# Small transfers of the normalisation and of the filter taps issued by GpSimd, filter taps written in pieces of 16 partitions, and the order of the work made with other costs

## The chip, the cores and the metric

The kernel runs on one core of a Trainium2 chip, whose cores have five engines with queues of their own: TensorE (PE, with its weight loads shown apart as PEld), VectorE (DVE), ScalarE (ACT), GpSimd (POOL) and SyncE (SP). Each engine executes its instructions strictly in the order in which they were written, and waits at an instruction until the semaphores named there have their values. A DMA is issued by an engine's queue (here SP, ACT or POOL) and carried out by the core's 16 DMA engines. The metric is the device time of one execution in microseconds; lower is better.

## The reference

The input `x` is 2048 positions by 448 channels, bf16. The result mixes an attention branch `a` and a state-space convolution branch `b` with a gate `g` of each position:

```
x = A_x
g = _sigmoid((x * gate_w).sum(-1, keepdims=True))
a = _A_ref(x, A_wq, A_wk, A_wv, A_wo)
b = _B_ref(x, B_A_re, ..., B_log_dt, B_Dskip)
return g * a + (1 - g) * b
```

`_A_ref` is attention with 16 heads of 28 channels that share one set of keys and values: `softmax(q k^T / sqrt(28)) v`, then a product with `wo`. `_B_ref` makes a filter `K` of 2048 taps for each of the 448 channels, from 256 complex states, and convolves each channel of `x` causally with its filter (there by FFT):

```
logdA = dt * A
P = jnp.exp(logdA[:, :, None] * l[None, None, :])
K = jnp.einsum("dn,dnl,dn->dl", Cc, P, dB).real
...
y = (lambda x, *d: x.transpose(*d))(y, 0, 2, 1) + u * Dskip[None, None, :]
```

## The kernel before

**Attention** runs in 16 rounds: round i takes a block of 512 queries (i // 4) and a group of four heads (i % 4). In a round, 64 score tiles of 128 keys by 512 queries are made by TensorE (L1031, into the PSUM tensor `psS`), exponentiated by ScalarE in sets of two or three tiles (L1047, `expT`), and multiplied with the values by TensorE (L1056), which adds up in the one PSUM bank `psB`. The values have a column of ones, so that one row of `psB` per head is the softmax denominator. At a round's end `norm(i)` copies `psB` to `acc` (L947, DVE), which frees `psB` for the next round. Then four DMAs gather the denominators (`denT<-acc`), DVE takes reciprocals (L952), one DMA writes them to a DRAM scratch (`R_scratch<-denT`), four read them back spread over partitions (`rdenB<-R_scratch`), and DVE multiplies (L956, `onT<-acc,rdenB`). `acc` is single, so L956 of a round has to come ahead of L947 of the next. The last round, 15, does this with TensorE instead. After rounds 3, 7, 11 and 15 the output projection with `wo` follows (L930, L997) and is added to the output `O` in SBUF (L939).

**The convolution** goes through 14 blocks c of 32 channels. DVE builds tables of powers for a block (`masters` and `tables`, L736 to L834), TensorE makes the taps from them (`kgen`, L851), DVE copies these to `kstg` (L861, L864), and DMAs write `kstg` to the DRAM scratch `KP_scratch` (slot name `kw`). The taps are read back as Toeplitz tiles: each block has two calls of `conv`, with four tiles each, 112 tile loads in all (`T<-KP_scratch`, 1072 KB each, in `tload`), into four buffers of `T`. TensorE multiplies a tile with `U`, the rearranged input (L893, 32 matmuls for each tile), DVE scales the result of a `conv` (L902, `cst`), TensorE transposes it (L913), and DVE adds it to `O` (L921).

**The order.** The code first lists all operations with their dependences, an estimated duration and a priority. `Prog.schedule` then plays them through with these estimates and so sets one fixed order for each engine; `emit` writes it out with the semaphore waits. A transfer's estimate is its own duration, plus `DMA_NS` (2200 ns), plus `extra`; transfers share one time line `dmafree`, and their issuer is held for 500 ns for each DMA. All DMAs that the prediction speaks of are issued by SP, whose queue is as strict as that of the other engines: a tile load behind an issue that waits is not issued either.

In the profile, every DMA has line 128 (`e.dma_start` in `Prog.dma`), so DMAs are told apart by their tensors. POOL does only early work: constants and the 16 copies that make `U` (L495).

## Time and profile before

| | us |
|---|---|
| median of 3 runs (641.67 to 643.77) | 643.0 |
| the profiled execution itself | 646.27 |
| its span in the profile | 644.5 |
| first exponential of the attention | 30.2 |
| copy of `acc` of the first and of the last round | 65.7 and 597.4 |
| last taps copied to `kstg` | 537.2 |

The profile gives for each engine the time in which it was busy, for each wait the engine and line that ended it, and a row for each instruction or run of like instructions with its start, its duration and the idle time ahead of it in brackets. The mean granted TensorE clock was 0.72 of the full clock. Slices in which the engines are busy do not tell which of them sets the pace, since three of them are busy for three quarters of the span or more; the waits do.

### The profile page before, as it was taken

The numbers are of one execution on the slowest core, as the hardware profiler recorded it, in microseconds if no ns is written. First come the engines' busy times: TensorE is split into PE (matmuls) and PEld (weight loads), VectorE is DVE, ScalarE is ACT, GpSimd is POOL, SyncE is SP. The second block draws the span as 40 slices with busy tenths as digits, with TensorE's granted clock in tenths as the row PEclk, the third lists the DMA queues.
The fourth block names the chain that finished last, engine by engine and source line by source line (L and its number), as shares of the span: only waits on it lengthen the run. The fifth ranks groups of instructions, "written<-read, shape, count | busy, mean of one in ns | idle before, by whom it ended". The sixth has DMA issues, their size and how long they took to land.

```text
span 644.5 us, 18460 instructions
## 1 busy us (share of the span) xinstructions
PE 516.5 (80%) x8219; PEld 224.3 (35%) x8234; DVE 471.0 (73%) x1028; ACT 490.6 (76%) x427; POOL 23.3 (4%) x36
## 2 busy tenths in 40 slices
PE   6598788889689776869689879798997888899642
PEld 5231132434233332424232434243341434343431
DVE  8989998989788896959778988969795961010310
ACT  4689998979779795959678979878796989787000
POOL 2740000000000000000000000000000000000000
PEclk9755585959789795958777976767596879555855
DMA  9510006496657148494672747593948172999695
GB/s 271 136 29 2 17 7 243 132 395 236 229 212 262 38 152 339 103 396 164 254 261 68 289 126 312 179 410 105 386 151 319 45 253 73 404 392 344 270 421 200
DMA packets 48686, 139.03 MB, mean 216 GB/s; under 512 B 25360, under 2 KB 31056, under 8 KB 34272
## 3 DMA queue, kind: packets, MB, share of 16 engines
q1 hardware_dynamic: 47952, 137.30, 58.7%
q8 instruction: 64, 1.05, 0.6%
q10 hardware_dynamic: 656, 0.57, 0.3%
q14 instruction: 14, 0.11, 0.0%
HBM read 133.81 MB, written 3.91 MB: 214 GB/s over the span
## 4 chain that ended last, share of the span: by engine, by line
DMA 32%; DVE 24%; PE 20%; ACT 11%; SPq 9%; issue 2%; ACTq 0%
DMA denT<-acc 14%; ACT expT L1047 11%; SPq L128 9%; DMA T<-KP_scratch 7%; PE psS L1031 7%; DMA R_scratch<-denT 5%; DMA rdenB<-R_scratch 4%; PE psB L1056 4%; DVE tab L812 3%; PE psX L893 2%; PE psS L893 2%; DVE tmp L814 2%; DVE tab L818 2%; DVE tab L816 2%; DVE tab L814 1%
## 5 line engine op out<-in xcount | busy, mean ns | idle before, releaser
L1047 ACT ACTIVATE expT<-psS 128x1536 bf16<-128x1536 f32 (+1 forms) x410 | 475.6, 1269 | 89.9 <-PE psS L1031 88.0
L1031 PE MATMUL psS<-qT,kT 29*128 29x512 bf16 x1024 | 202.9, 493 | 38.6 <-ACT expT L1047 30.5
L1056 PE MATMUL psB<-expT,vaug 128*32 128x512 bf16 x1024 | 129.1, 495 | 1.0 <-DVE acc L947 1.0
L1031 PEld LDWEIGHTS psS<-qT,kT 29*128 29x128 bf16 x1024 | 40.6, 95 | 135.9 <-ACT expT L1047 90.6
L893 PE MATMUL psX<-T,U 128*18 128x128 bf16 (+7 forms) x1792 | 50.2, 262 | 33.0 <-DMA T<-KP_scratch 24.6
L812 DVE TENSOR_TENSOR tab<-tab,mbf 128x256 bf16<-128x256 bf16 (+4 forms) x70 | 68.4, 977 | 0.3
L893 PE MATMUL psS<-T,U 128*18 128x128 bf16 (+7 forms) x1792 | 55.7, 273 | 15.4 <-DMA T<-KP_scratch 15.1
L1056 PEld LDWEIGHTS psB<-expT,vaug 128*32 128x32 bf16 x1024 | 27.3, 97 | 87.5 <-issue 84.2
L893 PEld LDWEIGHTS psX<-T,U 128*18 128x18 bf16 (+7 forms) x1792 | 35.8, 112 | 50.7 <-DMA T<-KP_scratch 29.4
L851 PE MATMUL psX<-tab 128*32 128x64 bf16 x1280 | 50.8, 290 | 2.6 <-DVE tab L834 2.5
L893 PEld LDWEIGHTS psS<-T,U 128*18 128x18 bf16 (+7 forms) x1792 | 38.8, 115 | 36.7 <-issue 15.0
L952 DVE RECIPROCAL denT<-denT 128x16 f32<-128x16 f32 x15 | 3.8, 252 | 58.4 <-DMA denT<-acc 58.4
L851 PEld LDWEIGHTS psX<-tab 128*32 128x32 bf16 x1280 | 36.8, 138 | 19.3 <-issue 13.3
L814 DVE TENSOR_TENSOR tmp<-tab,mbf 128x256 bf16<-128x256 bf16 (+3 forms) x56 | 36.3, 649 | 0.0
L947 DVE COPY acc<-psB 128x512 f32<-128x512 f32 x16 | 11.0, 685 | 31.4 <-PE psB L1056 31.3
L829 DVE TENSOR_TENSOR tab<-tab,tmp 128x4096 bf16<-128x4096 bf16 x14 | 31.9, 2282 | 0.0
L814 DVE TENSOR_TENSOR tab<-tab,mbf 128x4096 bf16<-128x4096 bf16 x14 | 31.9, 2276 | 0.0
L902 DVE TENSOR_TENSOR cst<-psX,omq 128x512 bf16<-128x512 f32 x14 | 9.6, 686 | 26.4 <-PE psX L893 26.3
L736 DVE TENSOR_TENSOR msq<-mst 128x256 f32<-128x256 f32 x63 | 26.2, 415 | 0.0
L825 DVE TENSOR_TENSOR tmp<-tmp,mbf 128x64 bf16<-128x64 bf16 (+4 forms) x70 | 25.0, 357 | 0.4
L816 DVE TENSOR_TENSOR tab<-tab,tmp 128x128 bf16<-128x128 bf16 (+3 forms) x56 | 22.4, 400 | 0.2
L818 DVE TENSOR_TENSOR tab<-tab,tmp 128x128 bf16<-128x128 bf16 (+3 forms) x56 | 22.3, 399 | 0.0
(139 smaller groups left out, 458.9 us busy)
## 6 DMA issues: line engine op xcount, KB each, us to landing
T<-KP_scratch SPq DMA_DIRECT2D x112, 1072.0 KB, 8.7
rdenB<-R_scratch SPq DMA_DIRECT2D x60, 64.0 KB, 2.2
tab<-in_A_x_dram SPq DMA_DIRECT2D x4, 448.0 KB, 6.0
tab<-in_A_x_dram SPq DMA_DIRECT2D x16, 112.0 KB, 2.6
out_dram<-O SPq DMA_DIRECT2D x3, 448.0 KB, 3.8
denT<-acc SPq DMA_DIRECT2D x60, 2.0 KB, 6.7
KP_scratch<-kstg SPq DMA_DIRECT2D x56, 17.0 KB
tab<-in_A_x_dram SPq DMA_DIRECT2D x16, 56.0 KB, 6.3
```

The lines of the kernel that those rows point to most:

```text
L128: return [e.dma_start(o, i, **kw) for o, i in pairs]
L736: pg.op("dve", lambda e, k=k: e.tensor_tensor(msq.v(0, P, 0, [[BW, 2], [1, BW]]), both(k - 1), both(k - 1), ALU.mult), el(2 * BW), rd=keys ...
L812: vo(lambda e, dst=dst, src=src, mr=mr: e.tensor_tensor(dst, src, mr, ALU.mult), 2 * n, done + mk(lv), [kr, ki])
L814: vo(lambda e, src=src, mi=mi, w=w, tb=tb, to=to: e.tensor_tensor(tb.v(0, P, to, [[w * EW, 2], [EW, w], [1, EW]]), src, mi, ALU.mult), 2 * ...
L816: vo(lambda e, do=do, n=n, tb=tb, to=to: e.tensor_tensor(tab.v(0, P, do, [[1, n]]), tab.v(0, P, do, [[1, n]]), tb.v(0, P, to + n, [[1, n]] ...
L818: vo(lambda e, do=do, n=n, tb=tb, to=to: e.tensor_tensor(tab.v(0, P, do + BLK, [[1, n]]), tab.v(0, P, do + BLK, [[1, n]]), tb.v(0, P, to, ...
L829: vo(lambda e: e.tensor_tensor(tab.v(0, P, FM, [[64, 2], [EW, 32], [1, 64]]), tab.v(0, P, lo + 31 * EW, [[BLK, 2], [-EW, 32], [1, 64]]), r ...
L851: r = e.matmul(G.v(32 * g, 32, 64 * jj, [[1, 64]]), tab.v(0, P, lo + comp * BLK + 64 + o, [[EW, 32]]), tab.v(0, P, fo, [[mo - fo, 2], [EW, ...
L893: r = e.matmul(ps.v(32 * j, 32 - 2 * n, 128 * k, [[1, 128]]), self.U.v(0, P, (4 * gi + j) * 32 + 2 * n, [[1, 32 - 2 * n]]), self.T.v(0, P, ...
L1031: r = e.matmul(self.psS.v(0, P, 512 * (bo + k), [[1, 512]]), kT.v(32 * h, DH + 1, 128 * kt, [[1, 128]]), qT.v(32 * h, DH + 1, 512 * (i % 2 ...
L1047: pg.op("act", lambda e: e.activation(expT.v(0, P, 512 * es, [[1, n]]), self.psS.v(0, P, 512 * bo, [[1, n]]), AF.Exp, scale=SQ), 100 + n / ...
L1056: r = e.matmul(self.psB.v(32 * h, 32, 0, [[1, 512]]), vaug.v(0, P, 32 * kt, [[1, 32]]), expT.v(0, P, 512 * (t % RING), [[1, 512]]), start= ...
```

## The change

The change has four parts. The tap writes `KP_scratch<-kstg` and the three transfers of the normalisation are issued by POOL instead of SP. The tap writes are cut otherwise: before, eight pieces, of which four have 17 partitions and four have 16; now eight pieces of 16 partitions, and one that carries row 16 of each of the four groups (32 runs of 64 taps). The scheduler's estimates are others: a POOL issue holds its engine for 1000 ns, a transfer of POOL doesn't wait for the transfers ahead of it, four transfers have 2000 ns more of latency, a tile load 2500 ns in place of 1500, the taps' matmuls 235 ns in place of 285, and four matmuls of the convolution 58 ns in place of 70. So the order of every engine is made anew. What is computed stays the same.

```diff
             if o.slot is not None:
-                free[e] = r + 500.0 * o.ndma
-                s = max(r, dmafree)
-                dmafree = s + o.ns
-                end = dmafree + self.DMA_NS + o.extra
+                free[e] = r + (1000.0 if e == "pool" else 500.0) * o.ndma
+                s = r if e == "pool" else max(r, dmafree)
+                end = s + o.ns + self.DMA_NS + o.extra
+                dmafree = max(dmafree, s) + o.ns
...
-                pg.op("pe", lambda e, mm=mm, comp=comp: mm(e, comp), 285, mode="c", rd=keys,
+                pg.op("pe", lambda e, mm=mm, comp=comp: mm(e, comp), 235, mode="c", rd=keys,
...
-        lst = []
+        ko = self.kstg
+        rs = ko.rs
+        lst = [(dram(self.KP, 32 * c * KW + 1024, [[8 * KW, 4], [KW, 8], [1, 64]]),
+                bass.AP(tensor=ko.h, offset=16 * rs, ap=[[32 * rs, 4], [64, 8], [1, 64]]))]
         for g in range(4):
-            for h, (r0, nr) in enumerate(((0, 17), (16, 16))):
-                lst.append((dram(self.KP, h * KH + (32 * c + 8 * g) * KW, [[64, nr], [KW, 8], [1, 64]]),
-                            self.kstg.v(32 * g + r0, nr, 0, [[64, 8], [1, 64]])))
-        pg.dma(lst, (1056, 128), "kw", rd=["kst", "kst2"], wr=[("KP", c)], pr=0)
+            for h in range(2):
+                lst.append((dram(self.KP, h * KH + (32 * c + 8 * g) * KW, [[64, 16], [KW, 8], [1, 64]]),
+                            ko.v(32 * g + 16 * h, 16, 0, [[64, 8], [1, 64]])))
+        pg.dma(lst, (1056, 128), "kw", rd=["kst", "kst2"], wr=[("KP", c)], pr=0, eng="pool", extra=2000)
...
-               (128, 2 * TW), f"T{s}", rd=[("KP", gi // 8), "pad"] + x, wr=[("T", s)], pr=1, extra=1500)
+               (128, 2 * TW), f"T{s}", rd=[("KP", gi // 8), "pad"] + x, wr=[("T", s)], pr=1, extra=2500)
...
-                pg.op("pe", mm, 70, mode="c", rd=[("T", s)] + [("U", q) for q in range(4)],
+                pg.op("pe", mm, 58, mode="c", rd=[("T", s)] + [("U", q) for q in range(4)],
...
-                   (128, 64), "dn", rd=["acc"], wr=["dn"], pr=0)
+                   (128, 64), "dn", rd=["acc"], wr=["dn"], pr=0, eng="pool", extra=2000)
...
-            pg.dma([(dram(self.R, i * 2048, [[16, P], [1, 16]]), dv)], (128, 64), "rw", rd=["dn"], wr=[("R", i)], pr=0)
+            pg.dma([(dram(self.R, i * 2048, [[16, P], [1, 16]]), dv)], (128, 64), "rw", rd=["dn"], wr=[("R", i)], pr=0, eng="pool", extra=2000)
...
-                   (128, 2048), "rdb", rd=[("R", i)], wr=["rd"], pr=0)
+                   (128, 2048), "rdb", rd=[("R", i)], wr=["rd"], pr=0, eng="pool", extra=2000)
```

The diff moves lines behind L864 down by three: L893 is L896 after the change, L902 is L905, L921 is L924, L947 is L950, L952 is L955, L956 is L959, L1031 is L1034, L1047 is L1050, L1056 is L1059.

**First place: the issuing queues.** SP's queue before, from the reciprocals' write of one round to the taps of the block behind it:

```order
L128 DMA R_scratch<-denT 128x16
L128 DMA rdenB<-R_scratch 32x512 x4
L128 DMA T<-KP_scratch 128x1x4288
L128 DMA KP_scratch<-kstg 17x8x64
L128 DMA KP_scratch<-kstg 16x8x64
```

The last two rows stand four times in turn before the next tile load. POOL's queue now, behind the copies that make `U`, for one round and the start of the next:

```order
L128 DMA denT<-acc 32x1x16 x4
L128 DMA R_scratch<-denT 128x16
L128 DMA rdenB<-R_scratch 32x512 x4
L128 DMA KP_scratch<-kstg 32x1x64
L128 DMA KP_scratch<-kstg 16x8x64 x8
L128 DMA denT<-acc 32x1x16 x4
```

These rows repeat to the end of POOL's queue. SP's queue holds the 112 tile loads one behind the other, from the first to the last, and behind them the output.

**Second place: DVE between the copy of `acc` and the reciprocal of the second round** (i = 1). Before:

```order
L947 COPY acc<-psB 128x512
L713 CAST qT<-psS 128x512
L814 TENSOR_TENSOR tab<-tab,mbf 128x4096
L952 RECIPROCAL denT<-denT 128x16
L816 TENSOR_TENSOR tab<-tab 128x2048
L818 TENSOR_TENSOR tab<-tab 128x2048
```

Now, from the row right behind the copy of `acc` on:

```order
L713 CAST qT<-psS 128x512
L814 TENSOR_TENSOR tab<-tab,mbf 128x4096
L821 COPY tmp<-mbf 128x64
L816 TENSOR_TENSOR tab<-tab 128x2048
L818 TENSOR_TENSOR tab<-tab 128x2048
L825 TENSOR_TENSOR tmp<-tmp,mbf 128x64
L825 TENSOR_TENSOR tmp<-tmp,mbf 128x128
L779 CAST mbf<-seedq 128x2x64
L825 TENSOR_TENSOR tmp<-tmp,mbf 128x256
L779 CAST mbf<-qst 128x2x64
L825 TENSOR_TENSOR tmp<-tmp,mbf 128x512
L955 RECIPROCAL denT<-denT 128x16
```

Nine rows of table work have moved ahead of this round's reciprocal. In other rounds it is fewer rows than before: the order now puts about the same amount of work there in every round.

**Third place: DVE's last instructions**, from the copy of `acc` of the last round on. `cst` is written once for each `conv`. Before:

```order
L947 COPY acc<-psB 128x512
L968 RECIPROCAL denT<-psS 128x16
L970 COPY rdenB<-denT 128x512
L979 TENSOR_TENSOR onT<-acc,psS 128x512
L902 TENSOR_TENSOR cst<-psS,omq 128x512
L939 SCALAR_TENSOR_TENSOR O<-psS,gt,O 128x448 x2
L921 TENSOR_TENSOR O<-O,psS 128x16x16
L939 SCALAR_TENSOR_TENSOR O<-psS,gt,O 128x448
L939 SCALAR_TENSOR_TENSOR O<-psX,gt,O 128x448
L921 TENSOR_TENSOR O<-O,psS 128x16x16
L902 TENSOR_TENSOR cst<-psX,omq 128x512
L921 TENSOR_TENSOR O<-O,psS 128x16x16
```

Two more pairs of L902 and L921 follow. Now the whole rest is:

```order
L950 COPY acc<-psB 128x512
L971 RECIPROCAL denT<-psS 128x16
L973 COPY rdenB<-denT 128x512
L905 TENSOR_TENSOR cst<-psX,omq 128x512
L982 TENSOR_TENSOR onT<-acc,psS 128x512
L942 SCALAR_TENSOR_TENSOR O<-psS,gt,O 128x448 x4
L924 TENSOR_TENSOR O<-O,psS 128x16x16
L905 TENSOR_TENSOR cst<-psX,omq 128x512
L924 TENSOR_TENSOR O<-O,psS 128x16x16
```

Before, the results of four calls of `conv` are taken up behind the last copy of `acc`; now those of two. On PE, 476 of the 3584 matmuls of L893 stood behind the last one of L1056 before, and 192 do now.

## The prediction

> **What bounds the kernel now.** I read the page's first part, then the rounds of attention, then who waits for whom. No engine is full, and three are nearly even:
>
> ```profile
> span 644.5 us, 18460 instructions
> PE 516.5 (80%) x8219; PEld 224.3 (35%) x8234; DVE 471.0 (73%) x1028; ACT 490.6 (76%) x427; POOL 23.3 (4%) x36
> ```
>
> The copies of `acc`, one a round, measure the pace, and stretches of the trace show what a round holds (columns: PE, PEld, DVE, ACT, POOL busy, granted clock, DMA share, GB/s):
>
> ```profile
> L947 DVE COPY acc<-psB x16: 677/682/692, 65.7 to 597.4; 128x512 f32<-128x512 f32 x16
> 527.79 0.69 DVE acc L947
> 351.00:384.00 33.00, 27.60 (x563) 13.89 (x564) 29.03 (x65) 28.84 (x26) 0.00 (x0) 0.90 0.51 175
> 528.00:561.00 33.00, 27.33 (x498) 12.04 (x502) 3.80 (x8) 28.83 (x26) 0.00 (x0) 0.71 0.64 243
> 561.00:597.00 36.00, 35.52 (x488) 13.48 (x478) 4.55 (x8) 28.90 (x25) 0.00 (x0) 0.50 0.98 374
> ```
>
> From the first copy to that at 527.8 there are 13 rounds in 462.1 us, 35.5 us each; the good rounds take 33.0, of which ACT and DVE each work 29. So the front consists of 13 rounds in which three engines need 28 to 30 us each and lose 5 to 6 to each other. Then come two rounds in which DVE has nearly nothing left to do, and 47 us after the last copy in which only the convolution is left. The waits, PE's and ACT's between 42 and 597 us, say where the loss is (us, times, longest):
>
> ```profile
> ACT expT L1047 <- PE psS L1031: 84.2, 85, 4.9
> PE psS L893 <- DMA T<-KP_scratch: 15.1, 6, 4.3
> PE psX L893 <- DMA T<-KP_scratch: 10.5, 4, 4.3
> PE psX L893 <- DVE kstg L864: 6.5, 4, 2.8
> PE psS L913 <- DVE O L939: 4.6, 2, 4.0
> PE psS L1031 <- DVE qT L707: 3.7, 2, 2.7
> DVE denT L952 <- DMA denT<-acc: 58.4, 14, 8.4
> DVE onT L956 <- DMA rdenB<-R_scratch: 16.0, 6, 8.4
> ```
>
> ACT loses 84.2 us to PE. PE, ahead of it, stands 25.6 us for tile loads and 14.8 us in the three rows for a late DVE. DVE stands 74.4 us for the normalisation's transfers.
>
> **Term 1: SP freed of the tap writes.** The long waits for tiles have one form:
>
> ```profile
> 228.17 11.60 SPq L128 DMA_DIRECT2D KP_scratch<-kstg  x8
> 239.82 1.17 SPq L128 DMA_DIRECT2D T<-KP_scratch  x2
> 245.76 1.04 PE L893 MATMUL psX<-T,U 128*32 128x128 bf16 x32 [4.27 <-DMA T<-KP_scratch]
> 277.94 1.04 PE L893 MATMUL psS<-T,U 128*32 128x128 bf16 x32 [3.85 <-DMA T<-KP_scratch]
> 316.48 0.62 PE L893 MATMUL psS<-T,U 128*32 128x128 bf16 x16 [4.25 <-DMA T<-KP_scratch]
> ```
>
> SP is held for 11.6 us by the eight tap writes, a tile load stands behind them, and PE waits 4.27 us for it, and with it ACT. The two other rows stand behind such a block too. With only tile loads on SP, a load is issued when its buffer comes free. All 25.6 us could go, or nothing if the loads are late for another reason; near the upper end, since the three rows alone make 12.4, I take **-18**. The tap writes themselves have cover: DVE's order has the taps of a block at least a round ahead of the use of its first tile, except in the first two blocks.
>
> Section "Issuing engines are not separate DMA queues" of the Trainium skill's page "DMA: Bandwidth & Descriptors" says that a second issuer saves only the sequencer's time, usually small beside the transfer. Here it isn't small (11.60 us for eight writes).
>
> **Term 2: DVE's wait for the normalisation.** How long the gather takes depends on what is ahead of it in SP's queue:
>
> ```profile
> 98.61 2.41 SPq L128 DMA_DIRECT2D denT<-acc  x4
> 100.44 1.70 DMA denT<-acc
> 127.58 2.58 SPq L128 DMA_DIRECT2D T<-KP_scratch  x4
> 130.21 2.53 SPq L128 DMA_DIRECT2D denT<-acc  x4
> 132.14 11.11 DMA denT<-acc
> ```
>
> With no tile load ahead 1.7 us, right behind four of them 11.1. No trace here shows a DMA issued by POOL, so both ends come from the nearest rows:
>
> ```profile
> L495 POOL COPY U<-tab x16: 1022/1072/1778, 17.0 to 39.3; 128x896 bf16<-128x896 bf16 x16
> L128 SPq DMA_DIRECT2D denT<-acc x60: 513/592/1415, 66.4 to 564.3; - x60
> seedw<-in_gate_w_dram ACTq DMA_DIRECT2D x1, 0.9 KB, 5.1
> denT<-acc SPq DMA_DIRECT2D x60, 2.0 KB, 6.7
> R_scratch<-denT SPq DMA_DIRECT2D x15, 8.0 KB, 5.1
> rdenB<-R_scratch SPq DMA_DIRECT2D x60, 64.0 KB, 2.2
> ```
>
> An issue costs between SP's 0.59 and 1.07, the copies that POOL made itself. A small transfer lands in 1.7 (alone) to 5.1 (0.9 KB on ACT's queue beside the big loads of SP). The gather: four issues and a landing, 4.1 to 9.4, middle 6.7. Behind it one issue, a landing, four issues, and a landing of 2.2 to 5.1: 6.9 to 15.5, middle 11.2.
>
> Against these stands the work that the new order puts there. For the second place of the order, DVE's rows before show the parts:
>
> ```profile
> 97.21 0.68 DVE L713 CAST qT<-psS 128x512 bf16<-128x512 f32 x1
> 97.81 2.28 DVE L814 TENSOR_TENSOR tab<-tab,mbf 128x4096 bf16<-128x4096 bf16 x1
> 102.16 0.25 DVE L952 RECIPROCAL denT<-denT 128x16 f32<-128x16 f32 x1 [2.07 <-DMA denT<-acc]
> 102.33 1.16 DVE L816 TENSOR_TENSOR tab<-tab 128x2048 bf16<-128x2048 bf16 x1
> 105.93 0.28 DVE L776 TENSOR_TENSOR qst<-qst 128x128 f32<-128x128 f32 x1
> ```
>
> Now the work from 97.21 to 100.1 and that from 102.33 to 105.93 stand ahead of the reciprocal, 6.2 us after small differences; before it was 2.9, and DVE stood for 2.07. The same sum over all 13 rounds, with DVE's own durations, gives 4.3 to 6.5, mean 5.0, ahead of the reciprocal, and 10.3 to 11.3, mean 10.8, from there to L956. So DVE stands 0 to 4.4 and 0 to 4.7 us a round, at the middles 1.7 and 0.4. That is 13 x 2.1 = 27 us instead of 74.4; at the upper ends 118. PE's 14.8 us for a late DVE shrink with it by two thirds, 9.4; with the smaller rows of the kind I take **-10**. Bounds: -15, and +44 (118 - 74) if DVE then sets the pace.
>
> By that section of the skill the gather would keep SP's 6.7 us of landing: 4 x 0.59 to 4 x 1.07 and 6.7, less 5.0, are 4.1 to 6.0 us a round, at most 78 us, so term 2 would be about 0 and the sum ten higher.
>
> **Term 3: more convolution among the attention.** 284 matmuls of L893 (476 less 192) now stand ahead of the last L1056. The row at 245.76 has 32 in 1.04 us, so this is 9.2 us of PE. It costs nothing where PE waits for ACT, and all of it at half clock, where PE is full (35.52 of 36.00). I take half, **+5**.
>
> **Term 4: the tail.** After 597 the tile loads set the pace:
>
> ```profile
> 589.52 35.93 SPq L128 DMA_DIRECT2D T<-KP_scratch  x13
> 612.87 0.69 DVE L902 TENSOR_TENSOR cst<-psX,omq 128x512 bf16<-128x512 f32 x1 [5.82 <-PE psX L893]
> 624.94 0.69 DVE L902 TENSOR_TENSOR cst<-psX,omq 128x512 bf16<-128x512 f32 x1 [10.21 <-PE psX L893]
> 635.14 0.69 DVE L902 TENSOR_TENSOR cst<-psX,omq 128x512 bf16<-128x512 f32 x1 [8.34 <-PE psX L893]
> ```
>
> 13 loads in 35.93 us, 2.76 each; a `conv` of four is 11.1 (12.1 and 10.2 between the last three `cst`). One tile serves 32 matmuls, so 284 fewer are 8.9 loads, 24.5 us. What is left behind the last copy, 1.5 convs, takes 16 us, longer than the last round's own projection, so loads still set the end. Between 0 (if the loads in the last round fall as far behind) and 24.5 I take **-22**: the last two rounds hold 4.3 convs now as before, so the loads should be no more behind. What is late next is then the output's DMAs, unchanged.
>
> **Sum.** -18 - 10 + 5 - 22 = -45 on the span of 644.5: 599.5. The profiled execution took 646.27, 1.8 outside its span, so 601.3; the median of the three runs, 643.0, stands 3.3 lower. **598 us**. A check from the other side: the front loses 23 of 13 rounds, 33.7 us a round, and good rounds of before took 33.0.
>
> **The rivals.**
>
> *PE at half clock takes the front's gain.* From 561 to 597 the clock was 0.50, PE was full, and the round took 36.0. If the rounds are held by PE, terms 1 and 2 give nothing and term 3 costs 9.2: 643.0 + 9.2 - 22 = 630. For it: that row. Against it: rounds at 0.71 to 0.90 took 33, and nothing in the change makes PE slower.
>
> *POOL's queue is no faster, and DVE stands longer than before.* At the upper ends 9.1 us a round instead of 5.7; DVE sets the pace of the front and adds 44 us, term 1 disappears in it, and the tail still gives 22 less 5: 643 + 44 - 17 = 670. It decides from about 7 us a round on: there 13 x 7 - 74 = 17 eats the tail's gain. The place to see it is L955 and L959. For it: 5.1 us for 0.9 KB on another queue, and four issues in a row twice a round. Against it: 1.7 us alone, and only the top of the range reaches it.
>
> *DVE's copies hold up POOL's issues.* A copy or cast of DVE lasts at most 0.7 us (0.68 above); once ahead of each of the two legs in each of 13 rounds it would add 18 us to DVE's waits, and 5 to 18 to the time: 603 to 616. No row before has POOL and such a DVE copy at work on one thing, so a small chance. Section "Who interferes with whom" of the Trainium skill's page "SBUF — State Buffer" is where it comes from: GpSimd, which writes descriptors itself, is locked out while DVE runs a copy, cast or tensor_scalar in a two-port mode, though not during a tensor_tensor. Were all DVE work to count, it would be far worse; that page denies it.
>
> *The order moves and the waits are made up elsewhere:* the time stays at 641 to 645.
>
> **How the numbers follow.** The forecast, most of it between 585 and 616, 0.55; DVE's copies in POOL's way, 0.05; PE-bound front or part of it, 616 to 641, 0.20; the same, 0.05; POOL too slow, 645 to 680, 0.15, half of it above 655. Within 0.3% (1.9 us, about what a measurement of this kernel can tell from no change) 0.05, so faster 0.80 (0.55 + 0.05 + 0.20), slower 0.15. The range goes from 583 to 655: some 0.10 of the forecast may lie below, should the rounds come to 32.5 us, and 0.08 above.
>
> **What would show it.** The waits of PE L896 for `T<-KP_scratch` ahead of the last round: 25.6 before, under 8 if term 1 is right. DVE's waits at L955 and L959: 74.4 before, 27 expected, over 90 if POOL is slow. The copies of `acc` 33 to 34 us apart, against 36 if PE holds them. From the last copy of `acc` to the end 25 us instead of 47. Wrong it would be made above all by POOL's issues of more than 1.5 us, or by a clock near 0.5 over the front.

## The result, and the profile after

| | before | after |
|---|---|---|
| median of the timed runs, us | 643.38 (641.67 to 644.01, 4 runs) | 610.87 (605.95 to 612.34, 4 runs) |
| ratio, with its 95% interval | | 0.9485 [0.9425, 0.9545] |
| the profiled execution, us | 646.27 | 612.23 |
| its span, us | 644.5 | 610.5 |
| first copy of `acc` to that of round 13, us | 462.1 | 452.1 |
| from there to the last copy of `acc`, us | 69.6 | 70.0 |
| last copy of `acc` to the end, us | 47.1 | 22.6 |

The changed kernel is faster by 5%. On the span that is 34.0 us: 10.0 from the 13 rounds in front, 24.5 from the tail, and 0.5 lost (0.4 in the last two rounds, 0.1 ahead of the first copy). A run that took over 1.5% more than the fastest of its kernel is left out of the ratios, here and below, but not out of the medians (one in `e2_order`, `e8_taps_pool_pe` and `e12_after_17`, two of the four in `e11_joined`). The profile of the changed kernel, its first part and then its costliest groups on POOL and the transfers' landings (last column of the latter: median us from issue to landing):

```profile
span 610.5 us, 18493 instructions
...
PE 506.3 (83%) x8234; PEld 222.4 (36%) x8234; DVE 471.5 (77%) x1028; ACT 490.6 (80%) x427; POOL 159.9 (26%) x297
...
L128 POOL DMA_DIRECT2D KP_scratch<-kstg x126 | 67.2, 541 | 110.5 <-DVE kstg L864 86.7
...
L128 POOL DMA_DIRECT2D denT<-acc x60 | 30.6, 514 | 131.0 <-DVE acc L950 128.2
...
L128 POOL DMA_DIRECT2D rdenB<-R_scratch x60 | 30.4, 512 | 74.2 <-DMA R_scratch<-denT 71.5
...
rdenB<-R_scratch POOLq DMA_DIRECT2D x60, 64.0 KB, 4.8
...
denT<-acc POOLq DMA_DIRECT2D x60, 2.0 KB, 4.4
```

DVE and ACT do the work of before to within half a microsecond; only their idle time went. An issue on POOL takes 0.51 to 0.57 us; on SP it was, in the median, 0.59 for the gather and 0.42 for the read back. The gather lands sooner than before (4.4 us against 6.7), the read back later (4.8 against 2.2).

The copies of `acc`, the row of all of them and then that of round 13 in DVE's timeline (start, duration):

```profile
L950 DVE COPY acc<-psB x16: 675/682/693, 65.8 to 587.9; 128x512 f32<-128x512 f32 x16
```

```profile
517.86 0.68 DVE L950 COPY acc<-psB 128x512 f32<-128x512 f32 x1
```

The 13 rounds take 34.8 us each, against 35.5 before. The waits between 42 and 600 us:

```profile
ACT expT L1050 <- PE psS L1034: 74.7, 92, 5.3
...
DVE onT L959 <- DMA rdenB<-R_scratch: 41.6, 12, 9.3
DVE denT L955 <- DMA denT<-acc: 29.6, 9, 7.4
...
PE psS L1000 <- DVE onT L959: 4.0, 1, 4.0
...
PE psX L896 <- DMA T<-KP_scratch: 3.2, 1, 3.2
```

PE's waits for tiles are nearly gone, 25.6 to 3.2 us. DVE's waits for the normalisation are not: 58.4 and 16.0 became 29.6 and 41.6, in sum 74.4 became 71.2. ACT still loses 74.7 us to PE.

**The front is DVE's.** The prediction took these waits over all 16 rounds. Over the stretch of the 13 rounds the windows give the busy time of the engines (PE, PEld, DVE, ACT, POOL), and the waits of DVE in the same stretch are its own. Before, windows and then waits:

```profile
65.70:527.80 462.10, 384.98 (x6317) 162.56 (x6330) 393.37 (x861) 386.58 (x335) 0.00 (x0) 0.75 0.58 209
```

```profile
DVE denT L952 <- DMA denT<-acc: 44.7, 12, 8.4
...
DVE onT L956 <- DMA rdenB<-R_scratch: 4.2, 4, 1.7
```

After:

```profile
65.80:517.90 452.10, 384.38 (x6644) 167.60 (x6643) 395.03 (x863) 387.05 (x335) 122.35 (x234) 0.79 0.65 236
```

```profile
DVE onT L959 <- DMA rdenB<-R_scratch: 26.4, 10, 5.4
DVE denT L955 <- DMA denT<-acc: 17.5, 7, 4.5
```

DVE works 393.4 us of 462.1 before and stands 48.9 at these two places: 442.3, and 19.8 us are left for everything else. After it is 395.0 + 43.9 = 438.9 of 452.1, with 13.2 left. So DVE has little other idle time, and the rounds are nearly as long as its work and its two waits. The rest of the 74.4, 25.5 us, lay in the last two rounds, where DVE has little else to do (27.3 after). These two rounds took 69.6 us before and 70.0 after, and one of the waits reached PE there: it stood 4.0 us for L959.

### The profile page after: what moved, and what is told of

Its sections match the earlier page's. It is cut to its first block, busy times and chain, and to the rows that moved or that the text cites. A ratio compares the mean times of both kernels' runs of the same rounds, so it can differ in the third digit from the quotient of the medians.

```text
span 610.5 us, 18493 instructions
## 1 busy us (share of the span) xinstructions
PE 506.3 (83%) x8234; PEld 222.4 (36%) x8234; DVE 471.5 (77%) x1028; ACT 490.6 (80%) x427; POOL 159.9 (26%) x297
## 4 chain that ended last, share of the span: by engine, by line
DMA 32%; DVE 27%; PE 19%; ACT 13%; POOL 5%; issue 3%; ACTq 0%; SPq 0%
ACT expT L1050 13%; DMA rdenB<-R_scratch 11%; DMA R_scratch<-denT 10%; DMA denT<-acc 8%; PE psS L1034 6%; DVE tab L812 4%; PE psB L1059 4%; POOL rdenB L128 3%; PE psX L896 2%; POOL denT L128 2%; DVE tab L814 2%; DVE tab L816 2%; DVE tmp L814 2%; PE psS L701 2%; DMA T<-KP_scratch 2%
## 5 line engine op out<-in xcount | busy, mean ns | idle before, releaser
L1050 ACT ACTIVATE expT<-psS 128x1536 bf16<-128x1536 f32 (+1 forms) x410 | 475.7, 1267 | 80.0 <-PE psS L1034 78.5
L1034 PE MATMUL psS<-qT,kT 29*128 29x512 bf16 x1024 | 199.0, 483 | 30.7 <-ACT expT L1050 29.1
L1059 PE MATMUL psB<-expT,vaug 128*32 128x512 bf16 x1024 | 127.0, 486 | 3.4 <-DVE acc L950 3.4
L128 POOL DMA_DIRECT2D KP_scratch<-kstg x126 | 67.2, 541 | 110.5 <-DVE kstg L864 86.7
L1034 PEld LDWEIGHTS psS<-qT,kT 29*128 29x128 bf16 x1024 | 40.5, 94 | 133.3 <-ACT expT L1050 86.1
L896 PE MATMUL psX<-T,U 128*32 128x128 bf16 (+7 forms) x2176 | 64.0, 265 | 10.6 <-DVE kstg L864 7.4
L128 POOL DMA_DIRECT2D denT<-acc x60 | 30.6, 514 | 131.0 <-DVE acc L950 128.2
L896 PEld LDWEIGHTS psX<-T,U 128*32 128x32 bf16 (+7 forms) x2176 | 46.5, 114 | 35.1 <-issue 19.5
L1059 PEld LDWEIGHTS psB<-expT,vaug 128*32 128x32 bf16 x1024 | 27.3, 96 | 87.2 <-issue 78.4
L128 POOL DMA_DIRECT2D rdenB<-R_scratch x60 | 30.4, 512 | 74.2 <-DMA R_scratch<-denT 71.5
L959 DVE TENSOR_TENSOR onT<-acc,rdenB 128x512 bf16<-128x512 f32 x15 | 10.4, 692 | 41.7 <-DMA rdenB<-R_scratch 41.6
L896 PE MATMUL psS<-T,U 128*32 128x128 bf16 (+7 forms) x1408 | 36.2, 245 | 6.5 <-DVE kstg L864 6.3
L851 PE MATMUL psS<-tab 128*32 128x64 bf16 x896 | 33.1, 289 | 7.6 <-DVE tab L834 7.5
L851 PE MATMUL psX<-tab 128*32 128x64 bf16 x896 | 33.6, 289 | 4.9 <-DVE tab L834 4.9
L896 PEld LDWEIGHTS psS<-T,U 128*32 128x32 bf16 (+7 forms) x1408 | 26.8, 105 | 18.8 <-issue 9.0
L851 PEld LDWEIGHTS psS<-tab 128*32 128x32 bf16 x896 | 25.4, 136 | 15.2 <-DVE tab L834 9.1
L851 PEld LDWEIGHTS psX<-tab 128*32 128x32 bf16 x896 | 25.5, 137 | 14.5 <-issue 6.8
```

The source lines that it names most:

```text
L128: return [e.dma_start(o, i, **kw) for o, i in pairs]
L851: r = e.matmul(G.v(32 * g, 32, 64 * jj, [[1, 64]]), tab.v(0, P, lo + comp * BLK + 64 + o, [[EW, 32]]), tab.v(0, P, fo, [[mo - fo, 2], [EW, ...
L896: r = e.matmul(ps.v(32 * j, 32 - 2 * n, 128 * k, [[1, 128]]), self.U.v(0, P, (4 * gi + j) * 32 + 2 * n, [[1, 32 - 2 * n]]), self.T.v(0, P, ...
L959: pg.op("dve", lambda e: e.tensor_tensor(ov, av, self.rdenB.v(0, P, 0, [[1, 512]]), ALU.mult), el(512), rd=["acc", "rd", "onw"], wr=[("on" ...
L1034: r = e.matmul(self.psS.v(0, P, 512 * (bo + k), [[1, 512]]), kT.v(32 * h, DH + 1, 128 * kt, [[1, 128]]), qT.v(32 * h, DH + 1, 512 * (i % 2 ...
L1050: pg.op("act", lambda e: e.activation(expT.v(0, P, 512 * es, [[1, n]]), self.psS.v(0, P, 512 * bo, [[1, n]]), AF.Exp, scale=SQ), 100 + n / ...
```

## The experiments

Each is timed in four runs (`e12_after_17` in ten) beside the kernel before on the same chip, where that took 642.3 to 643.6 us; the ratio is to that. Three things are taken apart: the queue, the cut of the taps, and the order. Where an engine's order is kept, it is kept row for row; only the issuer of a transfer or the cut of the taps differs (for that, the estimates count the nine writes of the new cut as eight in the order of before, and the eight of the old as nine in the order of after).

| | order | taps | normalisation | us, median | ratio, interval |
|---|---|---|---|---|---|
| before | before's | SP, 17 and 16 | SP | 643.4 | 1 |
| `e1_queues` | before's | POOL, 16 | POOL | 609.6 | 0.9483 [0.9437, 0.9529] |
| `e2_order` | after's | SP, 17 and 16 | SP | 653.6 | 1.0152 [1.0097, 1.0206] |
| `e3_taps_pool` | before's | POOL, 16 | SP | 602.8 | 0.9357 [0.9301, 0.9412] |
| `e4_pieces` | before's | SP, 16 | SP | 612.6 | 0.9532 [0.9488, 0.9576] |
| `e7_taps17_pool` | before's | POOL, 17 and 16 | SP | 659.6 | 1.0245 [1.0197, 1.0293] |
| `e12_after_17` | after's | POOL, 17 and 16 | POOL | 634.8 | 0.9882 [0.9845, 0.9919] |
| after | after's | POOL, 16 | POOL | 610.9 | 0.9485 [0.9425, 0.9545] |
| `e5_pe_costs` | new matmul costs only | POOL, 16 | POOL | 585.2 | 0.9098 [0.9044, 0.9153] |
| `e8_taps_pool_pe` | new matmul costs only | POOL, 16 | SP | 589.3 | 0.9142 [0.9094, 0.9191] |
| `e6_latencies` | new transfer estimates only | POOL, 16 | POOL | 609.3 | 0.9479 [0.9419, 0.9539] |
| `e9_tload` | after's estimates, tile load 1500 | POOL, 16 | POOL | 612.2 | 0.9532 [0.9450, 0.9615] |
| `e10_no_extra` | after's estimates, without the 2000 | POOL, 16 | POOL | 676.5 | 1.0533 [1.0462, 1.0604] |
| `e11_joined` | that of `e5_pe_costs` | POOL, 16 | POOL, joined | 602.9 | 0.9277 [0.9176, 0.9379] |

### Queue and order apart

`e1_queues` has the change's queues and pieces in the order of before; `e2_order` the changed order with the queues and pieces of before. The edits are at the end of `schedule`, and in `e1_queues` the new list of taps writes:

```diff
+        for i in order["sp"]:
+            if ops[i].slot in ('kw', 'dn', 'rw', 'rdb'):
+                ops[i].eng = "pool"
+        order["pool"] += [i for i in order["sp"] if ops[i].eng == "pool"]
+        order["sp"] = [i for i in order["sp"] if ops[i].eng == "sp"]
         self.order = order
```

```diff
+        for i in order["pool"]:
+            if ops[i].slot is not None:
+                ops[i].eng = "sp"
+        order["sp"] = sorted(order["sp"] + [i for i in order["pool"] if ops[i].eng == "sp"],
+                             key=lambda i: ops[i].begin)
+        order["pool"] = [i for i in order["pool"] if ops[i].eng == "pool"]
         self.order = order
```

> The order of before on PE, ACT and DVE, row for row; the tap writes and the normalisation's transfers are issued by POOL, the taps in pieces of 16. Theory A (the front gains because tile loads no longer stand behind other issues on SP, the tail because the new order has 2.2 convs fewer behind the attention): PE's 25.6 us of waits for tiles fall under 5, the tail from the last copy of acc stays at 47 us, 625 to 633 us. Rival O (the new order is what matters, the queue does nothing): 640 to 646 us.

> The order of after on PE, ACT and DVE, row for row; all transfers issued by SP as before, taps in pieces of 17 and 16, SP's issues in the order of their modelled starts. Theory A: the tail is 23 to 27 us as in after, but the waits for tiles come back (25 us or more), 620 to 632 us. Rival O: 606 to 615 us, as after.

609.6 and 653.6 us. The new order with the old queues and pieces is 1.0 to 2.1% slower than before (with all transfers back on SP, in an order of SP's that had to be made for this kernel), the queues and pieces alone carry the whole gain, and more than either theory gave them. In `e1_queues` the rounds took 32.6 us, but the tail was the old one, 45.8. In `e2_order` the tail was the new one, 23.0, and the rounds 37.3. DVE's waits in the 13 rounds of `e1_queues` (its lines are five further on than the changed kernel's):

```profile
DVE denT L960 <- DMA denT<-acc: 13.0, 5, 3.7
DVE onT L964 <- DMA rdenB<-R_scratch: 6.4, 4, 3.8
```

### The cut of the taps

`e3_taps_pool` moves only the taps to POOL, `e4_pieces` moves nothing and only cuts the taps as the change does, and `e7_taps17_pool` moves the taps in their old pieces. The edit of `e3_taps_pool`, against `e1_queues`:

```diff
-            if ops[i].slot in ('kw', 'dn', 'rw', 'rdb'):
+            if ops[i].slot in ('kw',):
```

> The order of before; only the tap writes are issued by POOL, in pieces of 16; the normalisation stays on SP. Theory A: the tap writes were what held SP, so this alone takes PE's waits for tiles from 25.6 to under 8 us, 625 to 635 us, and it is within 5 us of the kernel that moves all four transfers. Rival O: 640 to 646 us.

> The order of before, all transfers on SP; only the cut of the taps is changed (nine pieces, eight of 16 partitions). Theory A, with the queue as the cause: nine issues hold SP still for 5 us or more, the waits for tiles fall by less than half, 636 to 645 us. Rival P (the pieces of 17 partitions hold SP, the queue doesn't matter): SP is held for about 9 x 0.6 = 5.4 us instead of 9 to 11.6, the waits for tiles fall under 8 us, 625 to 635 us, as with the taps on POOL.

> The order of before, the tap writes on POOL but in the old pieces of 17 and 16 partitions; the normalisation on SP. Theory A (a piece of 17 hurts only because it holds the queue that issues it): SP is free, 600 to 607 us as with pieces of 16 on POOL. Rival P2 (a piece of 17 also holds up the transfers of other queues): the normalisation and the tiles stay late, 620 to 645 us.

602.8, 612.6 and 659.6 us. The cut alone, all on SP, is as good as the whole change, and better than the 625 to 635 us that were expected of it at best. The taps' issues on SP (min/median/max ns of one issue), before and then `e4_pieces`:

```profile
L128 SPq DMA_DIRECT2D KP_scratch<-kstg x113: 224/682/6219, 22.0 to 544.3; - x113
```

```profile
L128 SPq DMA_DIRECT2D KP_scratch<-kstg x127: 430/432/1637, 22.9 to 513.2; - x127
```

And one block of taps in the timeline of `e4_pieces`, to be read beside the 11.60 us of eight writes before:

```profile
249.38 5.12 SPq L128 DMA_DIRECT2D KP_scratch<-kstg  x9
```

In the mean of the 14 blocks, nine writes of the new cut hold SP for 5.0 us (4.4 to 6.0) and eight of the old for 8.0 (5.9 to 11.6), because single issues of the old took up to 6.2 us. The front of `e4_pieces` follows, windows and DVE's waits (L955 and L959 there too):

```profile
68.60:497.70 429.10, 373.75 (x6331) 160.35 (x6330) 393.32 (x860) 384.85 (x335) 0.00 (x0) 0.81 0.63 226
```

```profile
DVE denT L955 <- DMA denT<-acc: 19.1, 10, 3.1
DVE onT L959 <- DMA rdenB<-R_scratch: 4.0, 4, 1.3
```

DVE stands 23.1 us in place of 48.9, and the 13 rounds are 33.0 us shorter; 25.8 of these are DVE's waits. They fall mostly because the gather, which stands behind the tap writes on SP, is issued sooner: in the mean of the 13 rounds its first issue comes 0.15 us after the copy of `acc` in place of 1.6, and it lands 5.3 us after its last issue in place of 6.0.

On POOL the old pieces are slow too. For `e7_taps17_pool` and then `e3_taps_pool`, the queue of POOL (packets, MB, share of the 16 engines' span), the issues, and the landings:

```profile
q0 software_dynamic: 7168, 2.36, 5.6%
...
KP_scratch<-kstg POOLq DMA_DIRECT2D x56, 17.0 KB, 8.6
KP_scratch<-kstg POOLq DMA_DIRECT2D x56, 16.0 KB, 8.9
```

```profile
L128 POOL DMA_DIRECT2D KP_scratch<-kstg x112: 537/974/1522, 94.3 to 567.4; - x112
```

```profile
q0 software_dynamic: 4032, 1.91, 1.3%
...
KP_scratch<-kstg POOLq DMA_DIRECT2D x112, 16.0 KB, 5.9
```

```profile
L128 POOL DMA_DIRECT2D KP_scratch<-kstg x126: 528/531/743, 94.7 to 501.9; - x126
```

The same taps take 5.6% of the DMA engines' time in place of 1.3%, their issues 0.97 us in place of 0.53, and the pieces of 16 partitions between those of 17 land as late as these (8.9 us against 5.9). SP's gather, which has no tap write in its queue there, is waited for 51.0 us over the whole of `e7_taps17_pool` against 16.9 in `e3_taps_pool`. Two things could make it late: a tile load ahead of it on SP that waits for taps, or a slower transfer. In the mean of the 13 rounds its first issue comes 0.7 us later than in `e3_taps_pool`, most of it from one round in which it stands behind such a tile load, but it lands 5.8 us after its last issue in place of 3.9. So the pieces of 17 hold up transfers of other queues as well, and freeing SP of them is no cure.

`e12_after_17` undoes the cut alone in the changed kernel (the old list of eight writes, issued by POOL, in after's order).

> The changed kernel with one part undone: the taps in the old eight pieces of 17 and 16 partitions, still issued by POOL, every engine's order row for row that of the changed kernel. Theory C (the cut is what the change gains from; in the order of before the old pieces on POOL cost 57 us against the new ones): 645 to 670, rounds above 37 us, the gather lands later than 5 us in the median. Rival O (the changed order, made with longer latencies, covers slow tap writes): 611 to 625, rounds below 35.5.

634.8 us, between the two ranges: the cut alone is worth 24 us there, and 57 in the order of before (`e7_taps17_pool` to `e3_taps_pool`).

With the pieces of 16, moving the taps to POOL brings 10 us (`e4_pieces` to `e3_taps_pool`), and moving the normalisation as well loses 7 of them (`e3_taps_pool` to `e1_queues`). The best front of all is that of `e3_taps_pool`:

```profile
67.50:487.90 420.40, 360.46 (x6331) 156.46 (x6330) 392.50 (x860) 383.20 (x335) 62.31 (x117) 0.85 0.65 234
```

```profile
DVE onT L964 <- DMA rdenB<-R_scratch: 7.7, 7, 2.8
DVE denT L960 <- DMA denT<-acc: 6.5, 8, 1.4
```

392.5 + 14.2 = 406.7 of 420.4.

### The order: matmul costs against transfer estimates

`e5_pe_costs` has only the new matmul costs, with before's estimates for transfers, `e6_latencies` only the new transfer estimates; both have the change's queues and pieces. `e8_taps_pool_pe` is the first of them with the normalisation on SP.

```diff
-                pg.op("pe", lambda e, mm=mm, comp=comp: mm(e, comp), 285, mode="c", rd=keys,
+                pg.op("pe", lambda e, mm=mm, comp=comp: mm(e, comp), 235, mode="c", rd=keys,
...
-                pg.op("pe", mm, 70, mode="c", rd=[("T", s)] + [("U", q) for q in range(4)],
+                pg.op("pe", mm, 58, mode="c", rd=[("T", s)] + [("U", q) for q in range(4)],
```

> All four transfers on POOL in pieces of 16, the order made with the transfer costs of before but with the two matmul costs of after (235 and 58): 27.3 convs stand ahead of the last round's end, where before had 24.3 and after 26.5. Theory A (moving convolution ahead lengthens the rounds about as much as it shortens the tail): rounds of 33.5 to 35 us, tail 16 to 23 us, 598 to 612 us. Rival L (the longer transfer latencies lengthen the rounds of after, the matmul costs only shorten the tail): rounds of 32.3 to 33 us, tail 16 to 23 us, 578 to 592 us.

> The kernel after with the two matmul costs of before (285 and 70): only the transfer costs of the order are new, and 24.3 convs stand ahead of the last round's end as before. Theory A: rounds of 32.3 to 33 us, tail 45 to 48 us, 602 to 612 us. Rival L: rounds of 34.5 us or more, tail 45 to 48 us, 628 to 645 us.

> Like the kernel with the matmul costs of after and the transfer costs of before, but with only the tap writes on POOL and the normalisation on SP. Theory A: 5 to 10 us less than that kernel, as without the matmul costs (602.8 against 609.6): 590 to 605 us. Rival L: 571 to 585 us.

585.2, 609.3 and 589.3 us. The matmul costs shorten the tail from 45.8 to 16.5 us at 0.7 us a round (33.3 against 32.6). The new transfer estimates alone change nothing (609.6 to 609.3, tail 47.0). Together, in the changed kernel, they are 26 us worse than the matmul costs alone. So the first two kernels speak against one theory each, and neither holds for both. Where the normalisation is issued makes no clear difference in this order (589.3 against 585.2, intervals overlapping), though theory A had SP 5 to 10 us faster. The end of SP's queue of loads in the timelines shows the tail, the changed kernel first, then `e5_pe_costs`:

```profile
562.79 28.59 SPq L128 DMA_DIRECT2D T<-KP_scratch  x8
...
602.97 5.47 SPq L128 DMA_DIRECT2D out_dram<-O  x7
```

```profile
541.27 19.49 SPq L128 DMA_DIRECT2D T<-KP_scratch  x7
...
575.18 5.48 SPq L128 DMA_DIRECT2D out_dram<-O  x7
```

Two kernels put one of the changed transfer estimates back, and keep the matmul costs:

```diff
-               (128, 2 * TW), f"T{s}", rd=[("KP", gi // 8), "pad"] + x, wr=[("T", s)], pr=1, extra=2500)
+               (128, 2 * TW), f"T{s}", rd=[("KP", gi // 8), "pad"] + x, wr=[("T", s)], pr=1, extra=1500)
```

```diff
-                   (128, 64), "dn", rd=["acc"], wr=["dn"], pr=0, eng="pool", extra=2000)
+                   (128, 64), "dn", rd=["acc"], wr=["dn"], pr=0, eng="pool")
```

The second edit is `e10_no_extra`, where it stands at `kw`, `rw` and `rdb` too.

> The changed kernel with one number of the order put back: the tile load's latency, 1500 ns for 2500; the normalisation's and the taps' 2000 ns and the matmul costs stay as changed. Matmul costs alone gave 585.2, matmul costs with all the longer latencies 610.9. Theory T (the longer tile-load latency spoils the order that the matmul costs make, since it puts each conv and its results later against the rounds): 583 to 596, rounds 33.0 to 33.8 us. Theory N (the 2000 ns on the normalisation and the taps spoil it, since they put more of DVE's table work ahead of L955 and L959): 605 to 614, rounds 34.5 to 35. This order has 27.75 convs ahead of the last round's end (26.5 in the changed kernel), so the tail should be 14 to 18 us by both.

> The changed kernel with the other numbers put back: no 2000 ns on the normalisation's three transfers and the tap writes; the tile load keeps 2500 ns, the matmul costs stay as changed. Theory T: 605 to 614, rounds 34.5 to 35 us, as in the changed kernel. Theory N: 583 to 596, rounds 33.0 to 33.8. If both this and the kernel with only the tile load put back are at 605 or more, neither latency is the cause alone, and the orders simply scatter by some 20 us; if both are below 596, either of them is enough to spoil it only together with the other.

612.2 and 676.5 us. The first shows that the tile load's latency is not what costs the 26 us. The second is against both theories: without the 2000 ns the kernel is slower than before. Its windows and DVE's waits:

```profile
66.90:565.20 498.30, 383.95 (x6633) 169.21 (x6649) 395.48 (x863) 387.83 (x335) 122.61 (x234) 0.75 0.59 215
```

```profile
DVE onT L959 <- DMA rdenB<-R_scratch: 55.7, 12, 8.4
DVE denT L955 <- DMA denT<-acc: 37.2, 11, 7.3
```

395.5 + 92.9 = 488.4 of 498.3: the whole loss against the changed kernel's front, 46.2 us, is DVE's waits (92.9 against 43.9). Another 15.5 us go in the last two rounds (85.5 against 70.0), where PE stands 9.5 us for L959 in one wait and 10.7 us for a late L905 in another. What DVE works between L950 and L955, and from there to L959, goes with the waits in front (the mean of the 13 rounds from DVE's rows, time in which two rows overlap counted once; the lines of the other kernels accordingly):

| | work ahead of the reciprocal, us | work ahead of L959, us | both waits, us | 13 rounds, us |
|---|---|---|---|---|
| `e10_no_extra` | 3.6 | 7.6 | 92.9 | 498.3 |
| after | 5.3 | 11.0 | 43.9 | 452.1 |
| before | 6.6 | 10.7 | 48.9 | 462.1 |
| `e1_queues` | 6.6 | 10.7 | 19.4 | 424.0 |
| `e6_latencies` | 6.1 | 11.3 | 20.7 | 423.5 |
| `e5_pe_costs` | 9.1 | 10.0 | 22.8 | 432.9 |

The estimate of a transfer decides how much work the order puts beside it. The change takes the common time line of transfers (`dmafree`) away from POOL's, which makes them look shorter, and gives them 2000 ns back. Without these, too little work stands there: from the reciprocal to the landing of the read back it takes 11.9 us in the mean, 4.3 more than the 7.6 of work, and DVE stands for 4.3 a round at L959.

### Why the changed order waits longer for the read back

By work alone the changed kernel should wait less than it does at L959: 11.0 us of work there, as in `e1_queues` 10.7, but 26.4 us of waits against 6.4. From the end of the reciprocal to the landing of the read back it takes 12.5 us in the mean, and 10.4 in `e1_queues`. The difference goes with what is on the DMA engines at the time. Two rounds of the changed kernel, timelines of SP, POOL and DVE (start, duration, idle time ahead and what ended it):

```profile
213.52 3.17 SPq L128 DMA_DIRECT2D T<-KP_scratch  x4
...
220.68 2.25 POOL L128 DMA_DIRECT2D rdenB<-R_scratch  x4 [6.16 <-DMA R_scratch<-denT]
...
229.38 0.69 DVE L959 TENSOR_TENSOR onT<-acc,rdenB 128x512 bf16<-128x512 f32 x1 [5.05 <-DMA rdenB<-R_scratch]
...
314.27 4.99 SPq L128 DMA_DIRECT2D T<-KP_scratch  x3
...
327.45 1.98 POOL L128 DMA_DIRECT2D rdenB<-R_scratch  x4 [4.28 <-DMA R_scratch<-denT]
...
333.61 0.68 DVE L959 TENSOR_TENSOR onT<-acc,rdenB 128x512 bf16<-128x512 f32 x1
```

And the windows from the first read back on (the last three numbers: granted clock, DMA share, GB/s):

```profile
220.70:225.40 4.70, 4.01 (x72) 1.90 (x76) 3.63 (x17) 3.33 (x4) 2.23 (x4) 0.50 1.01 414
327.50:332.20 4.70, 4.70 (x93) 2.45 (x92) 4.70 (x21) 4.04 (x4) 1.93 (x4) 0.59 0.24 59
```

In the first, four tile loads were issued 4 to 7 us ahead, the DMA engines are full, the read back lands 6.4 us after its issue (median of the four), and DVE stands 5.05 us. In the second the loads were 8 us and more ahead, the DMA share is 0.24, it lands after 2.3 us, and DVE doesn't stand at all. The other rounds are alike: with the DMA engines busy for 0.6 of the time or less from the first read back's issue to 3 us after the last one's, it lands after 2.2 to 2.5 us, and with 0.98 or more after 4.5 to 6.5. In the mean of the 13 rounds that share is 0.81 in the changed kernel, and 0.51 in `e1_queues` (summed from the packets), whose row is

```profile
rdenB<-R_scratch POOLq DMA_DIRECT2D x60, 64.0 KB, 2.4
```

So the changed order lays the small read back beside the tile loads, of 1072 KB each. That the estimate without `dmafree` is the reason for this place was not tried by itself.

### Joining the transfers

`e11_joined` takes the order of `e5_pe_costs` and makes one DMA of the four gathers, and one of the four reads back:

```diff
-            pg.dma([(self.denT.v(32 * h, 32, 0, [[1, 16]]), self.acc.v(32 * h + 28, 1, 0, [[16, 32], [1, 16]])) for h in range(4)],
+            pg.dma([(dv, bass.AP(tensor=self.acc.h, offset=28 * self.acc.rs, ap=[[32 * self.acc.rs, 4], [16, 32], [1, 16]]))],
...
-            pg.dma([(self.rdenB.v(32 * h, 32, 0, [[1, 512]]), dram(self.R, i * 2048 + 512 * h, [[0, 32], [1, 512]])) for h in range(4)],
+            pg.dma([(self.rdenB.v(0, P, 0, [[1, 512]]), dram(self.R, i * 2048, [[512, 4], [0, 32], [1, 512]]))],
```

> The order of the kernel with only the matmul costs (585.2 us), row for row; the four gathers of the denominators are one DMA over 128 partitions, and so are the four reads back: 3 transfers a round on POOL in place of 9. Theory I (POOL's issues at 0.50 us each lie on the way on which DVE waits, 6 of them a round, 3 us; DVE waits 43.3 us for denT and rdenB in that kernel): DVE's two waits fall to 5 to 20 us and the time to 573 to 582. Rival (these waits are hidden behind ACT and PE, or the landing of one large transfer takes up what the issues give): 583 to 590, waits of DVE down or not. Slower than 591 if the joined gather, with only four source partitions, is carried out by fewer DMA engines and lands in 8 us or more.

602.9 us (592.3 to 610.5), slower than 585.2 (581.5 to 589.0). In its profile, of an execution of 592.3 us, DVE's two waits in the front did fall, from 22.8 to 13.3 us, but the stretch grew from 432.9 to 435.7: 26.5 us are left beside DVE's work and these waits, where the other kernels whose front is shown above have 10 to 14, and before 19.8. Most of the rest is DVE's other waits, all for PE: 24.8 us against 13.0 in `e5_pe_costs`, at a granted clock of 0.77 against 0.81. The joined gather lands after 6.0 us (5.4), the joined read back after 5.9 (3.1). Why PE was later, and why the runs scatter by 18 us, stays open. The Trainium skill's page "DMA: Bandwidth & Descriptors", section "Why a DMA increments its semaphore by 16 and not by 1", says that a DMA goes to as many engines as the largest number up to 16 that divides the outermost dimension of both its sides, which would be 4 for both of the joined transfers. The later landings agree; no view here shows the engines one by one.

## Why the time came out near, and which steps were wrong

598 us were predicted, with a range from 583 to 655, and 610.9 were measured. Of the terms:

**Term 1, SP freed of the tap writes, -18: the wrong cause.** The waits for tiles did go, 25.6 to 3.2 us, under the 8 that were named, and the block of eight writes of 11.6 us was rightly seen as the harm. But the step took the queue for the cause and did not price the new cut at all. The runs show the reverse: the cut without the queue gives 612.6, the queue without the cut 659.6. Nor were the tile waits what held the rounds. In `e4_pieces` PE still stood 17.3 us for tiles between 42 and 600 us, and the front was 33 us shorter:

```profile
PE psX L896 <- DMA T<-KP_scratch: 14.1, 12, 1.6
...
PE psS L896 <- DMA T<-KP_scratch: 3.2, 4, 1.1
```

The tap writes on SP cost time there by way of the gather behind them, which belongs to term 2.

**Term 2, DVE's wait for the normalisation, 74.4 to 27: the step that failed.** It fell to 71.2, and in the 13 rounds that count from 48.9 to 43.9. Two things in it were wrong. The way from the reciprocal to the read back was costed at a middle of 11.2 us in every round, whatever else is under way. It took 12.5 in the mean: the reciprocals' write landed after 5.2 us, where 1.7 to 5.1 was taken though its own row before gave 5.1, and the read back is laid beside the tile loads in the changed order. And means were set against means, though a round in which the transfer is late costs time and one in which it is early gives none back. So 26.4 us are lost at L959 where 0.4 x 13, 5 us, were expected. At L955, 17.5 us were lost against an expected 22. The work beside the transfers was counted rightly (5.0 and 10.8 us; 5.3 and 11.0 in the trace). The second thing is that the term was worth more than it was given: 47 us less of these waits were priced at 10, but in front of round 13 they are nearly all of what `e4_pieces` gains (25.8 of 33.0 us) and `e10_no_extra` loses. The two errors cancelled in part: 5.0 us fewer waits and 10.0 us of front.

**Term 3, convolution moved forward, +5:** the matmul costs alone, which move 3.0 convs (24.28 to 27.28 done at the last round's end), cost 9 us over 13 rounds (424.0 to 432.9); the 2.2 convs of the change would be 7 by that (8.9 x 2.2 / 3.0, an estimate). The size was near. What it didn't see is the price of the order as a whole: with the same queues and pieces the changed order's rounds take 34.8 us against 32.6 in the order of before, 28 us over 13. 24.5 of these are DVE's two waits (43.9 against 19.4), so they belong to term 2 as well.

**Term 4, the tail, -22:** -24.5. The `e1_queues` and `e5_pe_costs` tails, 45.8 and 16.5, show that the matmul costs do it, through the convs done ahead, as the step said.

**Sum:** terms 1 to 3 gave -23 ahead of the last copy, measured -9.5; the tail made up 2.5 of it. That the time came out near is in part luck. `e1_queues` splits the change: its queues and pieces, given -28 by terms 1 and 2 (the second with the new order's work beside the transfers), bring 34 us, mostly by the cut that no term priced; the order, given -17 by terms 3 and 4, brings nothing on top (609.6 to 610.9), because the rounds lose what the tail gains.

**The rivals.** PE at half clock is excluded: the front's granted clock was 0.79 (0.75 before). POOL too slow is excluded by issues of 0.51 to 0.57 us and a gather that landed sooner. DVE's copies in POOL's way would show in the issues on POOL; those of the gather took 0.51 us in the mean and none over 0.97. A time of 641 to 645, with the waits made up elsewhere, is excluded by 610.9, though the order's part of the change did just that. Rounds of 33 to 34 us were expected, and 34.8 came.

The rule that a second issuer saves only issue time (the Trainium skill, page "DMA: Bandwidth & Descriptors", section "Issuing engines are not separate DMA queues") was set aside in the prediction because of the 11.60 us. With pieces of 16 the runs agree with it better than the prediction did: the other queue is worth 10 us of 612.6 for the taps, and nothing or less for the normalisation.

## What to carry to other kernels

Look at the partition counts of the DMAs before thinking about which queue issues them: here pieces of 16, with the rows over that in a transfer of their own, gave as much as the whole change, and pieces of 17 were slow on either queue. Find the engine whose work and waits add up to the length of a stretch: its waits are what can be gained there, and they are summed over that stretch, not over the whole span. Set a transfer against its cover round by round, not mean against mean. An order made from estimates can lose more than the change that it goes with: the same queues and pieces ran between 585 and 677 us as the estimates were changed, so try these one by one, and look at how much work stands beside each transfer and what else is on the DMA engines then.

## What was not expected of the hardware

With pieces of 17 among them, a single tap write held its issuer for up to 6.2 us on SP and 1.5 on POOL (medians 0.68 and 0.97); with pieces of 16 and the one of four groups it was up to 1.6 and 0.74 (medians 0.43 and 0.53). The pieces of 17 delayed the writes of 16 partitions beside them (8.9 us to landing against 5.9) and made the gathers on another queue land later (5.8 us against 3.9). In the trace of `e7_taps17_pool`, POOL's queue has 224 packets of 4096 bytes and 952 of 1024 for 56 pieces of each kind, four and one for a piece of 17 and 16 for a piece of 16, and single packets take up to 2.05 us; in `e3_taps_pool` it has none of 4096, and none takes over 0.33 us. By the Trainium skill's page "DMA: Bandwidth & Descriptors", section "Why a DMA increments its semaphore by 16 and not by 1", 17 partitions would go to a single DMA engine and 16 to all. The packets and the times agree, though the trace does not name the engines. The exception that the section gives for some copies on GpSimd's queue, rounded-up shares on up to 16 engines, would be two partitions an engine here, an estimate; a packet of 4096 bytes holds four.

The granted clock in the front was 0.85 in `e3_taps_pool` and 0.75 before, though PE was busy for a larger share of the stretch (360.5 of 420.4 against 385.0 of 462.1), with the same order on PE. No run here says why, nor how much of the gain comes by it; DVE's two waits are 34.7 of the 41.7 us that the stretch lost.
